# Two attention units first, and idle-time identity products, in a TensorE-bound fp32 kernel

## The chip, the cores and the metric

The kernel runs on one core of a Trainium2 chip. The metric is the device time of one launch in microseconds. Each comparison runs both kernels in rounds on the same chip. A profile is one execution of the kernel; its span (736.8 us before) is 1.8 us shorter than the timed launch.

## The reference, cut to what matters

```python
def _attn_ref(r, k, v, w, u):                # B, H, S, D = 4, 8, 768, 48
    state = np.zeros((B, H, D, D))
    for t in range(S):
        cur = einsum('bhd,bhe->bhde', u * kt, vt)
        y[:, :, t] = einsum('bhd,bhde->bhe', rt, state + cur)
        state = w * state + einsum('bhd,bhe->bhde', kt, vt)

def _moe_ref(x, w_gate, w_val, w_out):       # x: 3072 x 384, d_ff 1536
    g, val = x @ w_gate, x @ w_val
    return (g * sigmoid(g) * val) @ w_out
```

The attention output, reordered to (B*S, H*D), is x. The weights arrive as 64-bit floats, so the kernel rounds them to 32 bits itself.

## The kernel before

The sequence is cut into 24 **units** (6 chunks of 128 steps by 4 batches). Stage s turns unit s (transposes its khat and rhat on TensorE), scores unit s-1, and makes the outputs and the state update of unit s-2. Two units make a pair; each pair has 12 gate/value **pieces** of 12 matmul records, then projections. The weights are rounded in 18 **chunks**, each on three engines in turn: ScalarE splits (mag and low part), VectorE merges, GpSimd adds. A piece f of the first two pairs needs chunks 2(f//2) and 2(f//2)+1.

```python
    def round_act():                       # split, ScalarE: two buffers each
        ...
            mags[n] = two.tile([P, WN], INT32, name="w_mag", tag="w_mag")
            lows[n] = two.tile([P, WN], INT32, name="w_low", tag="w_low")
            act.activation(mags[n][:].bitcast(FP32), hi.bitcast(FP32), AF.Abs, ...)
            act.activation(lows[n][:], lo.bitcast(UINT32), AF.Copy, ...)
    def round_dve():                       # merge, VectorE (L163, L164)
        ...
            dve.tensor_scalar(dst, hi, -(1 << 31), None, ALU.bitwise_and)
            dve.scalar_tensor_tensor(dst, mag, 3, dst, ALU.logical_shift_left, ALU.bitwise_or)
            load_weights()
    def round_pool():                      # sum, GpSimd (L172)
        ...
            pool.tensor_tensor(dst, dst, low, ALU.add)
    def own_product(i): ...                # GpSimd: rk = r*k, rk = rk*u (L187, L188); VectorE: sum to du
    def scale(i): ...                      # GpSimd: khat, rhat; then the next loads
    def diagonal(i):
        du = dus.pop(i)
        if i < 6:
            for h in range(H):
                act.activation(At[i % 2][:, h, :], ident[:], AF.Identity, scale=du[:, h : h + 1])
        else:
            pool.tensor_mul(At[i % 2][:], ident ..., du ...)
    def outputs(i): ...                    # TensorE y_ps; ScalarE copies it to xT
    def update(i): ...                     # TensorE u_ps; VectorE and, from chunk 1, GpSimd update Z
    def gate_value(g, f):
        ...                                # 3 matmuls with wg, 3 with wv, into gv (two buffers)
        act.activation(sg[:], gv[:, 0, :], AF.Sigmoid)
        dve.tensor_mul(sg[:], sg[:], gv[:, 0, :])
        dve.tensor_mul(hT[g][:, f, :], sg[:], gv[:, 1, :])
    ...
    for s in range(N + 2):
        if 1 <= s <= N:
            diagonal(s - 1)
        if s + 1 < N:
            if s > 0:
                own_product(s + 1)
            scale(s + 1)
        if s < N:
            turn(s)
        gap(s, 0)                          # R: one rounding step on each engine, F: one piece
        if 1 <= s <= N:
            scores(s - 1, 0)
            gap(s, 1)
            scores(s - 1, 1)
        gap(s, 2)
        if s >= 2:
            outputs(s - 2)
            if s % 2:
                queue((s - 3) // 2)
            gap(s, 3)
            update(s - 2)
        gap(s, 4)
```

## Time and profile before

| what | value |
|---|---|
| time, median of the first 3 runs | 736.71 us (736.28 to 738.16) |
| TensorE busy | 696.1 us, 94% of the span |
| first gate/value piece | 47.60 us |
| turn of unit 6, with 12 pieces done | 92.38 us |
| turn of unit 8, with 22 pieces done | 136.81 us |

Read it as a start-up in which TensorE waits and a dense stretch in which it doesn't. A microsecond counts when the dense stretch starts earlier or loses less.

### The profile page before, as it was taken

The numbers are of one execution on the slowest core, as the hardware profiler recorded it, in microseconds if no ns is written. First come the engines' busy times: TensorE is split into PE (matmuls) and PEld (weight loads), VectorE is DVE, ScalarE is ACT, GpSimd is POOL, SyncE is SP. The second block draws the span as 40 slices with busy tenths as digits, with TensorE's granted clock in tenths as the row PEclk, the third lists the DMA queues.
The fourth block names the chain that finished last, engine by engine and source line by source line (L and its number), as shares of the span: only waits on it lengthen the run. The fifth ranks groups of instructions, "written<-read, shape, count | busy, mean of one in ns | idle before, by whom it ended". The sixth has DMA issues, their size and how long they took to land.

```text
span 736.8 us, 10255 instructions
## 1 busy us (share of the span) xinstructions
PE 696.1 (94%) x4298; PEld 558.2 (76%) x4298; DVE 223.4 (30%) x443; ACT 165.1 (22%) x352; POOL 184.0 (25%) x159
## 2 busy tenths in 40 slices
PE   2669997999999999999999999999999999999997
PEld 2558886867788787787788787788788778777773
DVE  6755566302222132222132232222223212212120
ACT  2965652211111121111121122021111112011110
POOL 5974526430303030303033033032122211000000
PEclk9779998999999999999999999999999999999999
DMA  8974461120201010201021020111100000000000
GB/s 218 255 212 126 111 171 23 33 55 1 44 12 33 12 43 1 44 12 33 12 44 33 12 44 12 31 29 26 33 23 12 12 12 2 12 11 2 11 12 25
DMA packets 85768, 33.99 MB, mean 46 GB/s; under 512 B 76368, under 2 KB 79568, under 8 KB 85712
## 3 DMA queue, kind: packets, MB, share of 16 engines
q1 hardware_dynamic: 82256, 28.52, 16.5%
q10 hardware_dynamic: 3456, 4.72, 1.8%
q8 instruction: 36, 0.59, 0.3%
q14 instruction: 20, 0.16, 0.1%
HBM read 28.51 MB, written 4.72 MB: 45 GB/s over the span
## 4 chain that ended last, share of the span: by engine, by line
PE 88%; POOL 5%; issue 2%; DMA 1%; DVE 1%; ACT 1%; SPq 0%; POOLq 0%
PE gv L366 49%; PE o_ps L384 25%; PE y_ps L329 5%; PE s_ps L299 5%; PE tp L285 2%; PE u_ps L342 2%; DMA r_ld<-in_r_dram 1%; POOL rk L187 1%; POOL wo L172 1%; POOL wg L172 1%; POOL rhat L261 1%; POOL rk L188 1%; POOL khat L260 1%; ACT xT L333 1%; DVE wo L164 0%
## 5 line engine op out<-in xcount | busy, mean ns | idle before, releaser
L366 PE MATMUL gv<-xT,wg 128*128 128x256 f32 x864 | 215.5, 386 | 15.0 <-ACT xT L333 9.9
L366 PE MATMUL gv<-xT,wv 128*128 128x256 f32 x864 | 212.4, 382 | 0.0
L384 PE MATMUL o_ps<-wo,hT 128*128 128x384 f32 x576 | 197.0, 487 | 0.6 <-ACT o_sb L390 0.6
L366 PEld LDWEIGHTS gv<-xT,wg 128*128 128x128 f32 x864 | 159.8, 192 | 46.4 <-ACT xT L333 12.1
L373 DVE TENSOR_TENSOR sg<-sg,gv 128x256 f32<-128x256 f32 x144 | 60.5, 420 | 413.1 <-ACT sg L372 413.1
L366 PEld LDWEIGHTS gv<-xT,wv 128*128 128x128 f32 x864 | 165.9, 192 | 23.1
L384 PEld LDWEIGHTS o_ps<-wo,hT 128*128 128x128 f32 x576 | 107.8, 190 | 62.5 <-ACT o_sb L390 1.2
L372 ACT ACTIVATE sg<-gv 128x256 f32<-128x256 f32 x144 | 55.2, 384 | 402.9 <-PE gv L366 402.9
L355 POOL TENSOR_TENSOR Z<-Z,wL 96x384 f32<-96x384 f32 x16 | 16.1, 1008 | 359.4 <-DVE Z L354 359.4
L374 DVE TENSOR_TENSOR hT<-sg,gv 128x256 f32<-128x256 f32 x144 | 60.5, 420 | 4.9
L299 PEld LDWEIGHTS s_ps<-rT,kT 96*128 96x128 f32 x384 | 52.5, 204 | 6.3 <-ACT rT L293 0.3
L299 PE MATMUL s_ps<-rT,kT 96*128 96x128 f32 x384 | 52.8, 287 | 0.0
L303 DVE COPY_PREDICATED At<-mask,s_ps 128x512 f32<-128x512 int32 x48 | 34.3, 732 | 45.3 <-PE s_ps L299 45.3
L273 POOL TENSOR_TENSOR At<-ident,du 128x1024 f32<-128x1024 f32 x18 | 34.1, 1894 | 38.0 <-PE y_ps L329 38.0
L329 PE MATMUL y_ps<-At,v_ld 128*32 128x128 f32 x768 | 34.9, 273 | 0.0
L288 ACT ACTIVATE kT<-tp,own 96x512 f32<-96x512 f32 x48 | 30.1, 675 | 1.3 <-PE tp L285 0.5
L329 PE MATMUL y_ps<-rT,Z 96*32 96x128 f32 x480 | 30.2, 278 | 0.0
L329 PEld LDWEIGHTS y_ps<-At,v_ld 128*32 128x32 f32 x768 | 29.1, 109 | 0.9 <-issue 0.8
L187 POOL TENSOR_TENSOR rk<-r_ld,k_ld 128x384 f32<-128x384 f32 x24 | 27.6, 1148 | 4.3 <-DMA r_ld<-in_r_dram 4.3
L390 ACT COPY o_sb<-o_ps 128x384 f32<-128x384 f32 x24 | 11.5, 479 | 73.7 <-PE o_ps L384 73.7
L260 POOL TENSOR_TENSOR khat<-k_ld,kscale 128x384 f32<-128x384 f32 x24 | 24.0, 999 | 13.3 <-PE u_ps L342 13.3
L333 ACT COPY xT<-y_ps 128x384 f32<-128x384 f32 x24 | 11.5, 478 | 63.7 <-PE y_ps L329 63.7
(55 smaller groups left out, 341.2 us busy)
## 6 DMA issues: line engine op xcount, KB each, us to landing
k_ld<-in_k_dram SPq DMA_DIRECT2D x24, 192.0 KB, 2.8
r_ld<-in_r_dram SPq DMA_DIRECT2D x24, 192.0 KB, 3.3
w_bits<-in_moe_w_gate_dram SPq DMA_DIRECT2D x6, 768.0 KB, 6.9
w_bits<-in_moe_w_val_dram SPq DMA_DIRECT2D x6, 768.0 KB, 5.9
v_ld<-in_v_dram SPq DMA_DIRECT2D x48, 96.0 KB, 2.6
w_bits<-in_moe_w_out_dram SPq DMA_DIRECT2D x6, 768.0 KB, 4.4
out_dram<-o_sb ACTq DMA_DIRECT2D x24, 192.0 KB, 1.9
ub<-in_u_dram SPq DMA_DIRECT2D x1, 192.0 KB, 4.8
```

The lines of the kernel that those rows point to most:

```text
L187: pool.tensor_mul(rk[:], rl[:], kl[:])
L260: pool.tensor_mul(khat[i % 4][:], k_ld[i % 2][:], kscale[:])
L273: pool.tensor_mul(At[i % 2][:], ident[:].unsqueeze(1).to_broadcast([P, H, P]), du[:].unsqueeze(2).to_broadcast([P, H, P]),)
L288: act.activation(kT[i % 2][:, :, e, :], tp[0:D2], AF.Identity, scale=own[:, e : e + 1])
L299: pe.matmul(ps[:, n, :], kT[i % 2][:, a, e, :], turned[i][:, a, :], start=True, stop=True, skip_group_check=True,)
L303: dve.copy_predicated(At[i % 2][:, 4 * half : 4 * half + 4], mask[:].bitcast(INT32).unsqueeze(1).to_broadcast([P, HP, P]), ps[:],)
L329: pe.matmul(ps[32 * q : 32 * q + 32, cc, :], *rows[q][n], start=(n == 0), stop=(n == len(rows[q]) - 1), skip_group_check=True,)
L366: pe.matmul(gv[:, o, :].rearrange("p (i t) -> p i t", i=2), wt[:, c, P * f : P * (f + 1)], xT[:, 2 * g % NX : 2 * g % NX + 2, c, :], start ...
L372: act.activation(sg[:], gv[:, 0, :], AF.Sigmoid)
L373: dve.tensor_mul(sg[:], sg[:], gv[:, 0, :])
L374: dve.tensor_mul(hT[g][:, f, :], sg[:], gv[:, 1, :])
L384: pe.matmul(ps[:], hT[g][:, f, P * j : P * (j + 1)], wo[:, f, :], start=(f == 0), stop=(f == FC - 1),)
```

## The change

It means to start the dense stretch early. The first two units run back to back, their v is loaded before weight chunks 1 and 2, all diagonals go to GpSimd, and the count of out-of-range decays leaves the start-up. Products with the identity that nothing reads are meant to keep TensorE's clock up until the first piece. The table of what fills each gap is redrawn. Its core, with cuts:

```diff
+    load_weights()
+    load_v(0)
+    load_weights()
+    load_v(1)
+    load_weights()
...
+    def warm(n):
+        ps = ps_f.tile([P, 2, 2 * P], FP32, name="warm", tag="gv")
+        for _ in range(n):
+            pe.matmul(ps[:, 0, 0:P], ident[:], ident[:], start=True, stop=True)
+    warm(18)
...
     def diagonal(i):
-        if i < 6:
-            for h in range(H):
-                act.activation(At[i % 2][:, h, :], ident[:], AF.Identity, scale=du[:, h : h + 1])
-        else:
-            pool.tensor_mul(...)
+        pool.tensor_mul(...)
...
+    warm(14)
+    scale(0); scale(1); round_act(); round_act(); round_dve()
+    turn(0); warm(3); turn(1); warm(4)
+    diagonal(0); scores(0, 0); scores(0, 1); diagonal(1)
+    round_pool(); round_dve()
+    scores(1, 0); scores(1, 1); warm(4); round_pool()
+    own_product(2); scale(2); round_act()
+    outputs(0); outputs(1); warm(4); queue(0)
+    own_product(3); scale(3)
...
+    turn(2); feed(1); update(0); round_weights(); feed(1); update(1)
+    for s in range(3, N + 2):
...
+        if s == 12:
+            count_outside()
```

(The added calls stand on lines of their own in the kernel; they are joined here.)

More of the change, by code (lines that the diff above doesn't have):

```diff
@@ L203, in fast @@
     load(1)
-    for n in range(3):
-        load_weights()
-    make_identity(nc, ident[:])
+    load_weights()
[3 more added lines that the diff above has]
+    load_weights()
+    make_identity(nc, ident[:])
+    def warm(n):
[3 more added lines that the diff above has]
+    warm(18)
     pool.memset(own[:], 1.0)
@@ L234, in fast @@
             dve.reciprocal(rscale[:].rearrange("p h d -> p (h d)"), x)
-    dve.tensor_mul(
-        wL[:], sq[:, 7, :].unsqueeze(2).unsqueeze(3).to_broadcast([D2, HP, 2, D]),
-        own[:].unsqueeze(1).unsqueeze(3).to_broadcast([D2, HP, 2, D]),
-    )
+    own_product(0)
+    own_product(1)
     pool.memset(mask[:], 1.0)
@@ L244, in fast @@
     )
-    own_product(0)
-    own_product(1)
-    dve.tensor_tensor(bad[:], held[:], wcol[:], ALU.not_equal)
-    dve.tensor_reduce(badc[:], bad[:], axis=AX.X, op=ALU.add)
-    dve.memset(ones[:], 1.0)
-    n_ps = ps_a.tile([P, HP, P], FP32, name="n_ps", tag="a")
-    pe.matmul(n_ps[0:1, 0, 0:1], badc[:], ones[:], start=True, stop=True)
-    act.copy(outside, n_ps[0:1, 0, 0:1])
     turned = {}
@@ L261, in scale @@
         pool.tensor_mul(rhat[i % 2][:], r_ld[i % 2][:], rscale[:])
-        load_v(i)
+        if i >= 2:
+            load_v(i)
         if i + 2 < N:
@@ L268, in diagonal @@
         du = dus.pop(i)
-        if i < 6:
-            for h in range(H):
-                act.activation(At[i % 2][:, h, :], ident[:], AF.Identity, scale=du[:, h : h + 1])
-        else:
-            pool.tensor_mul(
-                At[i % 2][:], ident[:].unsqueeze(1).to_broadcast([P, H, P]),
-                du[:].unsqueeze(2).to_broadcast([P, H, P]),
-            )
+        pool.tensor_mul(
+            At[i % 2][:], ident[:].unsqueeze(1).to_broadcast([P, H, P]),
+            du[:].unsqueeze(2).to_broadcast([P, H, P]),
+        )
     def pair(t, a):
@@ L355, in update, with count_outside @@
             pool.tensor_mul(z[:], z[:], wL[:].rearrange("p a e d -> p a (e d)"))
+    def count_outside():
+        dve.tensor_tensor(bad[:], held[:], wcol[:], ALU.not_equal)
+        dve.tensor_reduce(badc[:], bad[:], axis=AX.X, op=ALU.add)
+        dve.memset(ones[:], 1.0)
+        n_ps = ps_a.tile([P, HP, P], FP32, name="n_ps", tag="a")
+        pe.matmul(n_ps[0:1, 0, 0:1], badc[:], ones[:], start=True, stop=True)
+        act.copy(outside, n_ps[0:1, 0, 0:1])
     hT = {}
@@ L411, in queue, with gaps @@
                 todo.append(parts.pop(0))
-    EARLY = [
-        ("R", "", "", "", "R"),
-        ("R", "", "R", "", ""),
-        ("R", "", "R", "", ""),
-        ("R", "", "RF", "F", "F"),
-        ("RF", "F", "RF", "F", "F"),
-        ("RF", "F", "RF", "F", "RF"),
-        ("RF", "F", "RF", "F", "RF"),
-        ("RF", "F", "RF", "F", "RF"),
-        ("RF", "F", "RF", "F", "RF"),
-    ]
-    def gap(s, n):
-        for what in EARLY[s][n] if s < len(EARLY) else ("F" * (3, 2, 2, 3, 2)[n]):
+    def gaps(s, n):
+        for what in EARLY[s][n] if s in EARLY else ("F" * (3, 2, 2, 3, 2)[n]):
             if what == "R":
@@ L431, in gap @@
                 feed(1)
+    EARLY = {
+        3: ("RF", "F", "RF", "", "F"),
+        4: ("RF", "F", "RF", "F", "RF"),
+        5: ("RF", "F", "RF", "F", "RF"),
+        6: ("RF", "F", "RFF", "F", "RF"),
+        7: ("RF", "F", "RFF", "F", "RF"),
+        8: ("RF", "F", "RFF", "F", "RF"),
+        9: ("RF", "F", "RFF", "F", "RF"),
+    }
+    warm(14)
+    scale(0)
+    scale(1)
+    round_act()
+    round_act()
+    round_dve()
+    turn(0)
+    warm(3)
+    turn(1)
+    warm(4)
+    diagonal(0)
+    scores(0, 0)
+    scores(0, 1)
+    diagonal(1)
+    round_pool()
+    round_dve()
+    scores(1, 0)
+    scores(1, 1)
+    warm(4)
+    round_pool()
+    own_product(2)
+    scale(2)
+    round_act()
+    outputs(0)
+    outputs(1)
+    warm(4)
+    queue(0)
+    own_product(3)
+    scale(3)
+    dve.tensor_mul(
+        wL[:], sq[:, 7, :].unsqueeze(2).unsqueeze(3).to_broadcast([D2, HP, 2, D]),
+        own[:].unsqueeze(1).unsqueeze(3).to_broadcast([D2, HP, 2, D]),
+    )
+    turn(2)
+    feed(1)
+    update(0)
     round_weights()
-    scale(0)
-    for s in range(N + 2):
-        if 1 <= s <= N:
+    feed(1)
+    update(1)
+    for s in range(3, N + 2):
+        if s <= N:
             diagonal(s - 1)
         if s + 1 < N:
-            if s > 0:
-                own_product(s + 1)
+            own_product(s + 1)
             scale(s + 1)
@@ L443, in fast @@
             turn(s)
-        gap(s, 0)
-        if 1 <= s <= N:
+        gaps(s, 0)
+        if s <= N:
             scores(s - 1, 0)
-            gap(s, 1)
+            gaps(s, 1)
             scores(s - 1, 1)
-        gap(s, 2)
-        if s >= 2:
+        gaps(s, 2)
+        if s >= 4:
             outputs(s - 2)
@@ L453, in fast @@
                 queue((s - 3) // 2)
-            gap(s, 3)
+            gaps(s, 3)
             update(s - 2)
-        gap(s, 4)
+        gaps(s, 4)
+        if s == 12:
+            count_outside()
     assert done["pool"] == NW
```

## The prediction

> **What bounds the kernel now.** I read the page from the top, then the chain of waits, then the order of events on each engine in the first 135 us. The page first: the 40 slices are 18.4 us each.
>
> ```profile
> PE   2669997999999999999999999999999999999997
> ...
> POOL 5974526430303030303033033032122211000000
> PEclk9779998999999999999999999999999999999999
> DMA  8974461120201010201021020111100000000000
> ...
> PE 88%; POOL 5%; issue 2%; DMA 1%; DVE 1%; ACT 1%; SPq 0%; POOLq 0%
> ```
>
> TensorE is full from the third slice to the end, with one dent near slice 7, and the chain that ended last is 88% TensorE. So the kernel is a dense TensorE stretch behind a start-up that is not TensorE's. The time can only fall by (a) starting the dense stretch earlier, (b) losing less inside it. The waits of TensorE up to 140 us say where it loses:
>
> ```profile
> PE t_ps L229 <- DVE pw L225: 7.9, 1, 7.9
> PE gv L366 <- ACT xT L333: 6.4, 2, 5.8
> PE n_ps L253 <- DVE ones L251: 5.5, 1, 5.5
> PE gv L366 <- DVE hT L374: 5.1, 2, 4.2
> ```
>
> The dense stretch begins with the first gate/value piece, at 47.60 us, and not warm: the first line below has 6 matmul records in 2.93 us; the same six take 1.49 us at the next piece, when the clock is full.
>
> ```profile
> 40.70 1.10 PE L329 MATMUL y_ps<-At,v_ld 128*32 128x128 f32 x32
> 47.60 2.93 PE L366 MATMUL gv<-xT,wg 128*128 128x256 f32 x6 [5.80 <-ACT xT L333]
> 50.32 2.77 PE L366 MATMUL gv<-xT,wv 128*128 128x256 f32 x6
> 52.88 1.26 PE L342 MATMUL u_ps<-v_ld,khat 128*96 128x96 f32 x8
> 53.98 1.49 PE L366 MATMUL gv<-xT,wg 128*128 128x256 f32 x6
> ```
>
> That start is late by program order, not by arithmetic. GpSimd runs without a pause from 16 to 49 us (9.8 to 9.9 of 10 us busy in 20-40), and unit 1's outputs stand behind the turns and scores of units 2 and 3; then ScalarE's copy to xT, ready to go at 41.8, sits until 47.09 behind a weight split (w_low) that waits for GpSimd. The second loss is the dent, read in GpSimd's order of events, where each row starts as the last ends:
>
> ```profile
> 109.34 1.24 POOL L355 TENSOR_TENSOR Z<-Z,wL 96x384 f32<-96x384 f32 x1 [10.79 <-DVE Z L354]
> 110.55 1.80 POOL L172 TENSOR_TENSOR wo<-wo,w_low 128x768 int32<-128x768 int32 x1
> 112.31 1.89 POOL L273 TENSOR_TENSOR At<-ident,du 128x1024 f32<-128x1024 f32 x1
> 114.17 1.72 POOL L187 TENSOR_TENSOR rk<-r_ld,k_ld 128x384 f32<-128x384 f32 x1
> 115.97 1.00 POOL L188 TENSOR_TENSOR rk<-rk,ub 128x384 f32<-128x384 f32 x1
> 116.92 1.00 POOL L260 TENSOR_TENSOR khat<-k_ld,kscale 128x384 f32<-128x384 f32 x1
> ```
>
> ScalarE's w_low waits 5.68 us for the weight sum behind these rows, the sigmoids stand behind w_low, and TensorE waits 0.83 + 4.25 us for hT and then runs cold until 129: some 2.7 us more. After 130 us it waits 4.2 us in all.
>
> [...] Work ending at 119.7, 31.1 and 41.8 lost the clock 2.3, 2.2 and 5.2 us later (read in 2 us stretches), and it came back 5.1 to 5.7 us after work resumed. [...] the weight merge of VectorE (L164) takes 0.96 us alone, 5.26 us at 109.76 beside GpSimd's run; GpSimd's product takes 1.0 us or 1.72, its weight sum 1.8 or 2.5.
>
> **The change, part by part.**
> 1. Start. Unit 0 and 1 run next to each other, before the turns and scores of units 2 and 3. The path to the first piece, from rows of the kernel before: weight chunk 1 landed at 13.8 (issued 7.59, 6.2 later); now v of unit 0 (192 KB) is ahead of it, 1.0 us at the 186 GB/s of 16-20 us: 14.9. Both splits on ScalarE to 16.6; kT and rT of unit 0, 1.6 us: 18.3. Scores 1.8 us warm and their predicated copies: about 21. VectorE merges chunk 1 (0.95 + 0.96 to 2.07): 23 to 24. GpSimd adds chunk 1 (1.8 to 2.5): 25 to 26.5. Then rk, khat, rhat of unit 2, 4.0 us: 29 to 30.5; the turn of rhat, 0.44 us, and the first piece starts at about **30.0**. That is 17.6 us earlier. The 4.9 us of diagonals for units 0 and 1 leave ScalarE (2.43 each) and cost GpSimd 1.9 each; the added products with the identity (47 of 128 columns, a transpose's 0.11 to 0.21 each) lie in waits, but for the last four, 0.4 to 0.9, which also end before rhat.
> 2. Work that moves behind that point: turn of unit 3 (0.87), scores of unit 2 (1.78), update of unit 0 (0.68): **3.3** us that must be given back.
> 3. The new wait. Counting what each stage emits, the early table asks for more pieces than there are added chunks: in stage 3 piece 2 waits for chunks 2 and 3. TensorE: from 30.0, two pieces (2.59 each), two updates (0.68 each), turn 0.87, scores 1.78: free at 39.2. GpSimd from 29.8: rk, khat, rhat of units 3 and 4 (4.0 each), diagonal 1.9, two sums (2.1 each): 41.8 and 44.0. The gate half can run between, the value half (1.3) ends at 45.3 instead of 41.8: 3.5 lost, and part of the clock, 1.5: **5.0**. Stage 4: GpSimd 1.9 + 4.0 + 4.2 to 54.1 against TensorE at 52.0: **0.8** lost. Stage 5: the diagonal waits for unit 2's outputs (56.4), then 1.9 + 4.0 + 2.1: chunk 7 at 64.4 against TensorE at 60.6: 2.5 lost and half of a cold spell, 1.3: **3.8**. One xT gap, 0.5. Sum **10.1**.
> 4. Compare at one place, unit 6's turn. After: 30.0 + work (10 pieces 25.9, four updates 2.7, turns 3 to 5 2.6, scores 2 to 4 5.3, outputs 2.1 = 38.6) + 10.1 = 78.7. Before: 92.38, with two more pieces done (5.2): 87.2. Gain **8.5** us.
> 5. From there. Stage 7 keeps the order that made the dent (Z product, sum, diagonal, rk, khat, rhat, sum, split, sigmoid): 13.6 us at the least after the update, against 10.4 of TensorE work that needs no new buffer; I let it cost what it cost, 7.8. The shift of pieces ahead of the outputs adds nothing there. One xT gap less (0.6) pays for the count product that TensorE now waits for at stage 12 (0.6, an estimate). Everything later is full TensorE in both.
> 736.7 - 8.5 = **728**.
>
> **The rivals.** (A) GpSimd takes it all back. It gains four units' diagonals that ScalarE had[...], and each stall then brings a full cold spell: some 734. For it: GpSimd's 9.9 of 10. Against: VectorE will have gaps, and TensorE's order no longer needs unit 3 early. (B) The dent goes, because stages 6 and 7 have six pieces rather than five and the clock stays warm: 7 us more, some 721. Against: the pieces were added before the update that starts the chain, not after. (C) The early start is worth its full 17.6 - 3.3 = 14.3 us because the sums arrive in time: 722. Against: the counts in part 3. (D) Transfers become the bound: chunk 7 at 64 us needs 8 chunks and 7 units, some 10.6 MB, 42 us at the 250 GB/s of the first 50 us: not the bound.
>
> **Range and chances.** The main path is 728; A pulls to 734, B or C to 721-722, both together to 715. I give 720.5 to 734.5. Two per cent is 722.0: that takes B or C nearly whole. Faster by over 2% 0.18, within 2% 0.80, slower 0.02.
>
> **What would show it.** Right: first piece at 28 to 32 us; TensorE waits of 2 to 4 us for GpSimd's weight sums (L172) between 38 and 66, absent before; unit 6's turn at 77 to 82; a stall of 3 to 5 us for hT in stage 7; identical tail. Wrong: a first piece after 34 (the start is bound elsewhere), no waits for the sums (C), no dent (B), or GpSimd rows stretched so that unit 6's turn comes after 84 (A).

Rival A's 734 has about 5 us, for GpSimd rows that run some 0.7 us longer for each of seven chunks. The longer rows are in the kernel before (a weight sum of 2.55 us at 24.01, the next 1.83 at 26.52); the cause for them was not shown.

## The result, and the profile after

| | before | after |
|---|---|---|
| median, 6 runs each | 737.14 us (736.28 to 738.16) | 735.93 us (734.71 to 736.44) |
| ratio | | 0.9982, 95% interval 0.9969 to 0.9994 |

The ratio is the mean time of one kernel's fast runs over that of the other's in the same rounds, so it isn't quite the ratio of the medians. The change is faster by 0.18%, which counts as the same at 2%, and it lies outside the predicted range.

The page of the changed kernel, the same rows:

```profile
PE   8887997999999999999999999999999999999997
...
POOL 6887634733030303030303033032032211000000
...
PEclk9989998999999999999999999999999999999999
DMA  8876632121020201020201021011100000000000
...
PE 84%; POOL 7%; DVE 3%; issue 3%; ACT 1%; DMA 1%; SPq 0%; POOLq 0%; DVEq 0%; ACTq 0%
```

TensorE's row is fuller at the left, but the identity products are in it. It now has a second dent, in the fourth slice (55 to 74 us). On the chain that ended last GpSimd has gone from 5 to 7% and VectorE from 1 to 3%. The waits of TensorE up to 150 us (total, times, longest):

```profile
PE gv L369 <- DVE hT L377: 6.3, 4, 4.2
PE gv L369 <- POOL wv L172: 5.3, 2, 3.6
PE gv L369 <- POOL wg L172: 3.4, 1, 3.4
```

The stall for hT is still there, 4.2 us long. The 5.8 us wait for xT is gone. New are 8.7 us of waiting for the weight sums. TensorE's own order of events shows where:

```profile
29.87 1.46 PE L369 MATMUL gv<-xT,wg 128*128 128x256 f32 x6
...
42.66 2.93 PE L369 MATMUL gv<-xT,wg 128*128 128x256 f32 x6 [3.40 <-POOL wg L172]
...
56.54 1.56 PE L369 MATMUL gv<-xT,wv 128*128 128x256 f32 x6 [1.71 <-POOL wv L172]
...
68.34 2.55 PE L369 MATMUL gv<-xT,wv 128*128 128x256 f32 x6 [3.56 <-POOL wv L172]
```

The first piece starts at 29.87, 17.7 us earlier than before, and warm in this execution (e1_nowarm shows that this was luck). Then pieces 2, 4 and 6 wait for their chunks, and after the two long waits the six records take 2.93 and 2.55 us in place of 1.46: the clock is lost as well (granted 0.50 from 41.5 to 48.3 us and from 68.8 to 72.2). The head start melts:

| place | before | after | ahead |
|---|---|---|---|
| first piece | 47.60 | 29.87 | 17.7 |
| same, less work moved behind it (3.3) | | | 14.4 |
| turn of unit 6 (before has 2 pieces, 5.2 us, more) | 92.38 - 5.2 = 87.2 | 83.55 | 3.6 |
| turn of unit 8, equal work | 136.81 | 133.85 | 3.0 |
| end of the span | 736.8 | 734.6 | 2.2 |

So 10.8 of 14.4 us go between 30 and 84 us. What sets the sums there shows in GpSimd's order of events (left: start and duration; in brackets its idle time and what ended it), and under it VectorE's around the first of those sums:

```profile
50.86 1.82 POOL L172 TENSOR_TENSOR wg<-wg,w_low 128x768 int32<-128x768 int32 x1
54.66 1.82 POOL L172 TENSOR_TENSOR wv<-wv,w_low 128x768 int32<-128x768 int32 x1 [1.98 <-DVE wv L164]
58.17 1.81 POOL L172 TENSOR_TENSOR wg<-wg,w_low 128x768 int32<-128x768 int32 x1 [1.68 <-DVE wg L164]
59.95 1.89 POOL L267 TENSOR_TENSOR At<-ident,du 128x1024 f32<-128x1024 f32 x1
...
66.48 1.80 POOL L172 TENSOR_TENSOR wv<-wv,w_low 128x768 int32<-128x768 int32 x1
```

```profile
51.78 0.42 DVE L377 TENSOR_TENSOR hT<-sg,gv 128x256 f32<-128x256 f32 x1
52.12 0.54 DVE L190 TENSOR_REDUCE du<-rk 128x8 f32<-128x384 f32 x1
52.58 0.94 DVE L163 TENSOR_SCALAR wv<-w_bits 128x768 int32<-128x768 int32 x1
53.56 0.96 DVE L164 SCALAR_TENSOR_TENSOR wv<-w_mag,wv 128x768 int32<-128x768 int32 x1
```

The sum at 54.66 waited for the merge at 53.56. That merge stood behind the multiply at 51.78, which belongs to piece 3, and piece 3 had itself been late because of the sums before it. A late sum delays a piece, whose multiply delays the next merge, which delays the next sum. Between the last two sums above lie the diagonal of unit 4 and the four products of unit 6, whose turn comes only at 83.55.

### The profile page after: what moved, and what is told of

Same layout as the page of the kernel before. It is cut to its first block, busy times and chain, and to the rows that moved or that the text cites. A ratio compares the mean times of both kernels' runs of the same rounds, so it can differ in the third digit from the quotient of the medians.

```text
span 734.6 us, 10389 instructions
## 1 busy us (share of the span) xinstructions
PE 705.0 (96%) x4392; PEld 565.9 (77%) x4392; DVE 226.3 (31%) x443; ACT 151.9 (21%) x304; POOL 196.2 (27%) x165
## 4 chain that ended last, share of the span: by engine, by line
PE 84%; POOL 7%; DVE 3%; issue 3%; ACT 1%; DMA 1%; SPq 0%; POOLq 0%; DVEq 0%; ACTq 0%
PE gv L369 47%; PE o_ps L387 26%; PE s_ps L293 5%; PE y_ps L323 4%; PE tp L279 2%; PE u_ps L336 1%; POOL khat L257 1%; POOL rk L187 1%; POOL rhat L258 1%; POOL rk L188 1%; POOL At L267 1%; POOL wv L172 1%; DVE wo L164 1%; DMA r_ld<-in_r_dram 1%; POOL wg L172 1%
## 5 line engine op out<-in xcount | busy, mean ns | idle before, releaser
L267 POOL TENSOR_TENSOR At<-ident,du 128x1024 f32<-128x1024 f32 x24 | 46.1, 1923 | 38.0 <-PE y_ps L323 38.0
L293 PEld LDWEIGHTS s_ps<-rT,kT 96*128 96x128 f32 x384 | 49.7, 194 | 5.0 <-ACT rT L287 0.9
L293 PE MATMUL s_ps<-rT,kT 96*128 96x128 f32 x384 | 50.0, 277 | 0.7 <-ACT rT L287 0.7
L187 POOL TENSOR_TENSOR rk<-r_ld,k_ld 128x384 f32<-128x384 f32 x24 | 26.0, 1085 | 4.4 <-DMA r_ld<-in_r_dram 4.4
L258 POOL TENSOR_TENSOR rhat<-r_ld,rscale 128x384 f32<-128x384 f32 x24 | 25.6, 1068 | 0.0
L188 POOL TENSOR_TENSOR rk<-rk,ub 128x384 f32<-128x384 f32 x24 | 24.5, 1023 | 2.8 <-DMA ub<-in_u_dram 1.0
```

The source lines that it names most:

```text
L187: pool.tensor_mul(rk[:], rl[:], kl[:])
L188: pool.tensor_mul(rk[:], rk[:], ub[:])
L258: pool.tensor_mul(rhat[i % 2][:], r_ld[i % 2][:], rscale[:])
L267: pool.tensor_mul(At[i % 2][:], ident[:].unsqueeze(1).to_broadcast([P, H, P]), du[:].unsqueeze(2).to_broadcast([P, H, P]),)
L293: pe.matmul(ps[:, n, :], kT[i % 2][:, a, e, :], turned[i][:, a, :], start=True, stop=True, skip_group_check=True,)
```

## The experiments

All have 5 rounds and give correct results, except where said. There are 4 to 6 runs of each. Three jobs of four kernels ran on three chips; each has its own runs of the kernel before (medians 736.64, 736.00 and 736.71 us), so figures are compared across jobs by their ratio to before. One interval is some 0.0015 to each side (1.1 us). A difference of two ratios times 736.7 gives the microseconds below, good to about 1.5.

**Theory.** The start is early, but the weight sums, on GpSimd, set the pace of the pieces until unit 6, and the change itself loaded GpSimd. **Rivals:** the warm clock is what counts; the order of GpSimd's work is at fault, not its amount; the stall of stage 7 takes all gains.

| run | what | median us | ratio to before |
|---|---|---|---|
| (the change) | | 735.93 | 0.9982 |
| e1_nowarm | change without identity products | 737.22 | 1.0004 |
| e2_before_warm | before, with 25 products ahead of its first piece | 735.30 | 0.9971 |
| e3_diag_act | change, diagonals 2 to 5 on ScalarE | 730.88 | 0.9909 |
| e4_first_chunks | change, first pair reads only chunks 0 and 1 (wrong) | 730.61 | 0.9909 |
| e5_low3 | change, third buffer for the low part | 729.17 | 0.9907 |
| e6_order | change, sums ahead of the next unit's products | 750.03 | 1.0187 |
| e7_order_act | e6 and e3 | 742.61 | 1.0082 |
| e8_order_low3 | e6 and e5 | 751.14 | 1.0202 |
| e9_low3_act | e5 and e3 | 724.19 | 0.9827 |
| e10_lead | e9, rounding one chunk ahead | 730.18 | 0.9915 |
| e11_before_warm_low3 | e2 and e5's buffer | 728.91 | 0.9897 |
| e12_diag_twice | change, diagonals 2 to 5 made twice | 743.95 | 1.0093 |

### e1_nowarm

```diff
     def warm(n):
+        return
```

> The changed kernel without any of its 47 products. Theory S (the weight sums of GpSimd set the pace until stage 6, so what TensorE does before 42 us has slack): the first piece starts later or cold, by 1 to 3 us, but piece 2 still waits for the sum that ended at 42.6 us, and the time moves by less than 1.5 us (735 to 737). Rival W (the warm clock is worth its microseconds): first piece cold, +2.7 us, and start +1 us, both reach the end: 738.5 to 740.

Measured 737.22 us, ratio 1.0004: 0.0022 or 1.6 us slower than the change. That lies just past the first theory's limit, is about the size of the noise, and is far from the rival's 2.5 to 4. The first piece started at 31.11, cold (2.56 us for the first six records), and yet the gap to the change at unit 6's turn was 0.5 us (84.07 against 83.55): the wait for chunk 2 had shrunk from 3.40 to 1.00 us. What TensorE does before 42 us has slack.

A cold first piece is no mark of this run, though. Ten profiled kernels have all 47 products and the change's start (e10 slightly reordered). In the change and in e7 the first six records took 1.46 us; in the other eight, 2.28 to 2.77, as in e3:

```profile
29.38 2.57 PE L373 MATMUL gv<-xT,wg 128*128 128x256 f32 x6
```

There TensorE had idled for 1.7 us before unit 2's turn, as in the change, and the granted clock fell to 0.50 from 29.6 to 33.0. So the products didn't keep the clock up reliably, and the warm start in the change's profile was luck. This run therefore compares two starts that may both be cold, and says little of what a reliably warm one is worth.

### e2_before_warm

```diff
             outputs(s - 2)
+            if s == 3:
+                warm(25)
             if s % 2:
```

> The kernel before with 25 products (about 0.22 us each warm, 5.5 us) ahead of its first piece, where TensorE idled from 41.8 to 47.6: the second half of the change alone. If the clock is all that was lost there: the first piece runs in about 2.7 us in place of 5.3 and the end comes 2.5 us earlier, 734 to 735. Rival: what follows in stages 4 to 7 waits for weight sums and the stall of stage 7 takes it back: within 0.7 us of before.

The first piece starts at 47.66 as before, but warm:

```profile
47.66 1.56 PE L371 MATMUL gv<-xT,wg 128*128 128x256 f32 x6 [1.03 <-ACT xT L338]
```

The time falls by 2.1 us (0.9971), about the 2.7 us that the cold spell had cost. Products alone, in the old order, do as well as the whole change.

### e3_diag_act

```diff
     def diagonal(i):
         du = dus.pop(i)
+        if 2 <= i < 6:
+            for h in range(H):
+                act.activation(At[i % 2][:, h, :], ident[:], AF.Identity, scale=du[:, h : h + 1])
+            return
         pool.tensor_mul(
```

> The changed kernel with the diagonals of units 2 to 5 back on ScalarE (8 products of 0.3 us each), as before. Theory L (the load on GpSimd delays the sums): each sum of stages 3 to 5 comes 1.9 us or more earlier, the waits of TensorE for L172 fall from 8.7 to under 4 us and the time falls by 3 to 6 us, 730 to 733. Theory O (the order does: sums stand behind the next unit's products, merges behind the multiplies of the piece that waits): under 1.5 us.

Measured 730.88: 5.4 us faster than the change by the ratios, as the load theory says. TensorE's waits for sums fall less than it said, from 8.7 to 6.2 us and not to under 4. Piece 2 no longer runs cold, but in this profile piece 0 does, so the piece that meets the slow clock differs between the two profiles (piece 2 at 2.93 us for six records in the change, piece 0 at 2.57 here). The sum of chunk 7 starts at 62.46 in place of 66.48:

```profile
62.46 1.82 POOL L172 TENSOR_TENSOR wv<-wv,w_low 128x768 int32<-128x768 int32 x1 [1.06 <-DVE wv L164]
```

The turn of unit 6 is at 80.90, 2.65 us earlier, and that of unit 8 at 129.68, 4.2 us earlier. GpSimd still waits for merges, so load was not the only delay.

### e4_first_chunks

```diff
-                    wt[:, c, P * f : P * (f + 1)], xT[...]
+                    wt[:, c, P * (f % 2) : P * (f % 2 + 1)] if g == 0 else wt[:, c, P * f : P * (f + 1)], xT[...]
```

> Wrong on purpose: the first pair's 12 pieces read the columns of the first two chunks, so none waits for a later sum; all rounding is done as before. If the waits for the sums and the cold clock after them are where the gain went (8.7 + about 4.6 us): unit 6's turn at 69 to 72 in place of 83.6 and a time near 722 to 725. If other queues (w_low on ScalarE, merges on VectorE) hold the pieces as long: above 731.

Wrong (relative error 0.36). All waits for L172 vanish, and TensorE reaches the turn of unit 5 at 55.68 in place of 62.44. But the time falls by only 5.4 us, and unit 6's turn is at 80.07, not at 69 to 72. From ScalarE's order of events, then from TensorE's:

```profile
67.67 0.90 ACT L154 ACTIVATE w_low<-w_bits 128x768 int32<-128x768 uint32 x1 [5.19 <-POOL wv L172]
...
70.57 0.48 ACT L327 COPY xT<-y_ps 128x384 f32<-128x384 f32 x1
```

```profile
71.10 2.93 PE L369 MATMUL gv<-xT,wg 128*128 128x256 f32 x6 [5.05 <-ACT xT L327]
```

The split of chunk 9 needs the buffer that the sum of chunk 7 frees, so ScalarE stands for 5.19 us, with two sigmoids and the copy of unit 3's outputs behind it. GpSimd's chain reaches TensorE by this second path even when no piece reads its sums. My first theory for this run missed that path; the rival had named it, and the time lies next to the rival's 731.

### e5_low3

```diff
-    NX = 12
+    NX = 10
...
-            lows[n] = two.tile([P, WN], INT32, name="w_low", tag="w_low")
+            lows[n] = three.tile([P, WN], INT32, name="w_low", tag="w_low")
```

> The changed kernel with a third buffer for the low part of the weight split (room for it from xT, 10 units in place of 12); the order of every engine is the same. Theory Q (ScalarE's w_low waits for the sum two chunks back and holds the sigmoids and xT copies behind it): the stall of 4.2 us in stage 7 and the cold clock after it go, some 6 to 7 us: 728 to 730. Rival (GpSimd's own chain from the Z product sets that stall, the split only stands beside it): within 1.5 us of the change.

Measured 729.17, ratio 0.9907: 5.5 us faster than the change. The stall of stage 7, TensorE's order of events in the change and then in this run:

```profile
118.32 2.90 PE L369 MATMUL gv<-xT,wg 128*128 128x256 f32 x6 [4.24 <-DVE hT L377]
```

```profile
113.39 1.53 PE L369 MATMUL gv<-xT,wg 128*128 128x256 f32 x6 [1.25 <-DVE hT L377]
```

The wait falls from 4.24 to 1.25 us and the records stay warm. Of the gain 1.3 us is there at unit 6's turn (82.25), the rest comes after it. The order of every engine was the same; only the buffer differed (with it, xT holds 10 units instead of 12, which was not run alone).

### e6_order, e7_order_act and e8_order_low3

```diff
     for s in range(3, N + 2):
+        early = done["pool"] < NW
+        if early:
+            sums(); merge()
         if s <= N:
             diagonal(s - 1)
+        if early:
+            sums()
         if s + 1 < N:
             own_product(s + 1)
             scale(s + 1)
...                                   # splits and further merges between turns, scores and updates
```

> The changed kernel from stage 3 on with the same work in another order: the sums and merges ahead of the next unit's products, two chunks in each of stages 3 and 4, three after. Theory O (order): the sums of stage 3 end at about 36 and 42 in place of 42.6 and 44.4, the waits of TensorE for L172 fall under 4 us, time 726 to 731. Theory L (load alone): the products that now come later hold the turns instead; waits for khat and rhat take the place of the waits for the sums, and the time stays above 732.

> e6_order with the diagonals of units 2 to 5 on ScalarE. If load and order are two separate delays of one chain: 3 to 5 us less than e6_order. If the chain is no longer GpSimd's once the sums come first, ScalarE's extra 2.4 us a unit cost more than they bring: equal or slower than e6_order.

> e6_order with the third buffer of e5_low3. If the two waits add: e6_order less the gain of e5_low3, 720 to 725. If the order has already freed the splits: the same as e6_order within 1.5 us.

A clear miss: e6 took 750.03 us. Theory L's "above 732" covers the number, but not for its reason: the waits for khat hardly grew (3.5 us against 2.6). And the sums of stage 3 ended at 39.5 and 44.1, not at 36 and 42 as theory O had it. GpSimd's waits between 30 and 92 us:

```profile
POOL wg L172 <- DVE wg L164: 16.8, 3, 6.2
```

Put first in GpSimd's order, the sums stand waiting for their merges, 16.8 us in three waits, and the products that could have filled that time wait behind them. The loop of the last section got tighter, not looser. With the diagonals on ScalarE (e7) it is 742.61, 7.7 us better than e6, so load counts here too. The third buffer (e8) changes nothing, 751.14: there the splits are not what waits. A small part of the loss lies elsewhere: in e6, e7, e8 and e10 TensorE waits 2.1 us for the moved count at stage 12, which no other kernel with the moved count does. A sum ahead of its merge is no gain; I tried only this one order, so another order may still do better.

### e9_low3_act

The edits of e5 and e3 together.

> The changed kernel with both repairs that helped alone: third buffer for the low part (the change less 6.7 us) and the diagonals of units 2 to 5 on ScalarE (less 5). They act in different stages (7, and 3 to 5): if they add, 723 to 726. If the splits freed by the buffer had hidden the same wait, 727 to 729.

Measured 724.19, ratio 0.9827 (0.9814 to 0.9840), the fastest of all. From the change, e3 brought 5.4 us, e5 5.5 us, both together 11.4: they add. TensorE's waits up to 170 us: the sums still cost 6.2 us, hT 2.9 in place of 6.3.

```profile
PE gv L373 <- POOL wv L172: 6.2, 3, 2.8
...
PE gv L373 <- DVE hT L381: 2.9, 3, 1.3
```

### e10_lead

```diff
-    NX = 10
+    NX = 8
...
-            lows[n] = three.tile(
+            lows[n] = four.tile(
...
     warm(4)
-    round_pool()
+    round_act()
+    round_pool()
+    round_dve()
     own_product(2)
     scale(2)
-    round_act()
     outputs(0)
     outputs(1)
+    round_act()
     warm(4)
```

> e9 with the rounding one chunk ahead: chunk 2 is merged on VectorE before the outputs of unit 0, where VectorE idled, and a fourth buffer (xT 8 units) keeps the splits from waiting for the sums. If the sums wait for their merges: 2 to 4 us less than e9, 720 to 723. If GpSimd's load is what sets the pace: within 1.5 us of e9.

Slower than e9 by 6.5 us: 730.18. Both expectations missed (720 to 723, or within 1.5 us of e9). One chunk ahead, a sum comes up on GpSimd before its merge again:

```profile
63.33 1.82 POOL L173 TENSOR_TENSOR wv<-wv,w_low 128x768 int32<-128x768 int32 x1 [7.95 <-DVE wv L165]
```

GpSimd idled 7.95 us there, with unit 6's products behind. That this is the loss is not shown: GpSimd idles 6.29 us for a merge in e9 too (before the sum at 73.45), and unit 6's products were done at 69.8, long before its turn at 82.66. At that turn e10 is 4.7 us behind e9 but has one piece more done (2.6 us), so about 2 us are lost by then, near the noise. More is lost at stage 12, where TensorE waits for the moved count, which it doesn't in e9, and then runs cold:

```profile
280.60 0.19 PE L362 MATMUL n_ps<-ones,badc 96*1 96x1 f32 x2 [2.09 <-DVE ones L360]
...
281.64 4.44 PE L392 MATMUL o_ps<-wo,hT 128*128 128x384 f32 x8
```

The last eight records took 4.44 us; eight such records at 271.30 in e9 took 2.74. Wait and cold clock make 3.8 us. So this run is no clean test of the order, and xT of 8 units was not run alone either.

### e11_before_warm_low3

The edits of e2 and e5 on the kernel before.

> The kernel before with 25 products ahead of its first piece (as e2) and the third buffer (as e5), its old start and its diagonals on ScalarE. If the new start is worth nothing by itself, as e2 says: 727.5 to 729.5, no slower than e5. If the early start pays once the stall of stage 7 is gone: 731 or more, clearly slower than e5.

Measured 728.91, ratio 0.9897, against 0.9907 for e5: no slower. The new start, with the diagonals on GpSimd, is worth nothing even when the stall of stage 7 is out of the way.

### e12_diag_twice

```diff
-        pool.tensor_mul(At[i % 2][:], ...)
+        for _ in range(2 if 2 <= i < 6 else 1):
+            pool.tensor_mul(At[i % 2][:], ...)
```

> The changed kernel with the diagonals of units 2 to 5 made twice on GpSimd (1.9 us more in each of stages 3 to 6, the result the same): the suspected cost doubled. Load on the chain of sums: slower by 4 to 7 us, 739.5 to 743. If there is slack on GpSimd (it idles 2 to 8 us before some sums, for merges): slower by under 2 us.

Measured 743.95: 0.0111 or 8.2 us slower than the change, for 4 x 1.9 = 7.6 us more on GpSimd: the direction of the load theory, and past its 4 to 7. TensorE's waits up to 170 us:

```profile
PE gv L370 <- POOL wv L172: 7.1, 2, 5.6
PE gv L370 <- POOL wg L172: 5.9, 2, 4.1
```

The waits for sums grow from 8.7 to 13.0 us, and the clock is lost more often (0.91 against 0.95 over the first 160 us). Taking the same 7.6 us away (e3) brought 5.4. In stages 3 to 6 a microsecond on GpSimd cost 0.7 to 1.1 us of the kernel.

### What follows: the change in parts

| step, by the ratios | with two buffers | with three |
|---|---|---|
| identity products alone (e2 against before; with three: not run) | -2.1 us | |
| + early start and its table, diagonals 2 to 5 left on ScalarE (e3 against e2; e9 against e11) | -4.6 | -5.2 |
| + diagonals 2 to 5 on GpSimd (change against e3; e5 against e9) | +5.4 | +5.9 |
| sum | -1.3 | |

The row "early start" also holds the earlier v, the diagonals of units 0 and 1, the moved count and the new table, which weren't run apart. The 25 products of e2 stand elsewhere than the 47 of the change, so the first row is only about what those bring.

## Why the prediction was wrong

It said 728.0, in 720.5 to 734.5; the time is 735.93. The direction and the mechanism were right, most sizes up to 42 us too. Step by step:

1. **Start: right.** 30.0 predicted, 29.87 measured, and by the predicted path: chunk 1 was merged at 23.44 (23 to 24 predicted) and added at 25.42 (25 to 26.5), rhat of unit 2 was done at 29.33 (29 to 30.5). That the first piece then ran warm was luck. One input was off: a product with the identity took 0.39 us at first (18 in 7.08 us) and about 0.24 us later (14 in 3.32), not 0.11 to 0.21. They lay in waits all the same.
2. **Work that moves (3.3 us): right** by the places both kernels pass.
3. **"Sum 10.1": this is the step that failed.** Measured from the first piece to unit 6's turn: 53.68 us less 38.6 of work is 15.1.

| term | predicted | measured, how |
|---|---|---|
| stage 3, piece 2 | 5.0 | 6.3: wait 3.40, and 2.87 because pieces 2 and 3 took 8.05 us for 5.18 |
| stage 4, piece 4 | 0.8 | 1.7: wait |
| stage 5, piece 6 | 3.8 | 5.3: wait 3.56, and 1.76 cold |
| xT gap | 0.5 | 0.6 |
| small starts | 0 | 1.2, the rest |

I added GpSimd's rows as if each sum could start when GpSimd was free: chunk 5 at 54.1, chunk 7 at 64.4. They ended at 56.5 and 68.3. The sums of chunks 5 and 6 waited 1.98 and 1.68 us for merges, which stood behind the multiplies and copies of late pieces in VectorE's order; some rows ran longer, with a merge of VectorE under way as they began (a sum 2.53 us at 40.08, the next 1.82; a diagonal 2.61 at 44.35, the next 1.89). And I halved the cold spells: one came whole (2.87 us for 1.5), the other as 1.76 for 1.3. The chain is not GpSimd's alone: it goes round through TensorE, ScalarE and VectorE, and every lateness is handed on.

4. **"Gain 8.5": 3.6,** which is the error of step 3.
5. **"From there", zero: -1.4.** The stall of stage 7 came as predicted (0.83 + 4.24 us, then cold). But there were two small new waits for hT, 0.41 us at 91.97 and 0.82 at 139.20, so "everything later is full TensorE in both" wasn't so. The count product, put at 0.6, cost no wait here.

Steps 3 and 5 make 6.4 us of the 7.9 that the prediction missed; most of the rest is that the two profiled spans differ by 2.2 us and the timed means by 1.3.

Three readings of the kernel before were off, none of which carries the error. Unit 1's outputs stood behind the turns of units 2 and 3 but the scores of unit 2 only; those of unit 3 came at 60.07. While the copy to xT sat from 41.8 to 47.09, only 1.12 us was a wait for GpSimd's sum; most of the time went to the splits themselves, some 0.9 us each. And in steps of 0.2 us the clock came back 5.0, 5.6 and 6.2 us after work resumed.

**The rivals.** A, "GpSimd takes it all back", said 734 and came nearest; of its reasons, e3 and e12 show the diagonals (5.4 us less and 8.2 more); the longer rows of GpSimd were read from durations, and no run tried them alone. I had argued against it that VectorE would have gaps; it had them, but in the wrong places, before merges whose turn hadn't come. B fell: the stall stayed until a buffer was added. C fell: the sums weren't in time, and e4 shows that even pieces which don't need them would have been held by ScalarE. D was right to be set aside; no transfer of weights held a sum of the changed kernel between 30 and 70 us.

**Still open.** How much the cold spells cost by themselves was read from durations, not tried. Whether an order of sums and merges exists that does better than e9 is open too; two tries (e6, e10) were worse, of which e10 lost more at stage 12 than in the order. What the smaller xT costs wasn't run, nor what a first piece that is always warm would bring.

## What to carry to other kernels

A head start at the bottleneck engine is worth what its next inputs are early by: before advancing it, follow the second and third item it will ask for, through every engine that makes them. Moving work from an engine with room to the one that paces those inputs can cost most of its duration: here 5.4 of 7.6 us, about as much as the reordering (4.6) had won. A short buffer ring that lets one engine's queue wait for another engine, with unrelated work behind (5.19 us on ScalarE in e4), is cheap to look for and here was worth 5.5 us.

## What the traces show of the clock and the merges

- In the kernel before the clock came back 5.0 to 6.2 us after work resumed. The cold spells themselves (granted 0.50), read in steps of 0.2 to 0.4 us, lasted 6.8 us there (33.3 to 40.1, 47.0 to 53.8) and 3.4 us in e3 (29.6 to 33.0).
- Nearly equal waits had different outcomes: the wait before piece 6 cost the clock in e3 (2.82 us; six records then took 2.93 us) and not in e9 (2.83 us; 1.56 us). A gap of 1.7 us came before the cold first piece of e3.
- The granted clock doesn't account for every slow record: in the changed kernel it reads 1.00 from 1 to 8 us, while the products took 0.39 us each, against 0.24 later.
- The merge that took 0.96 us at 53.56 in the changed kernel, with GpSimd idle, took 5.26 us at 104.17, while three GpSimd instructions ran in a row (103.74 to 108.6). Why it took so long the runs don't show.
